# Hash-masked attention with a channel mix: the opening rearranged head by head, pair 1 turned by TensorE, and the plan of hand-overs shifted

## The chip, the cores and the metric

The kernel runs on one core of one Trainium2 chip. The time is the device time of one execution in microseconds (us). Every kernel was run several times; medians are given with the lowest and highest run. The kernel before takes 291.65 us (three runs, 291.47 to 292.93).

Each execution also has a label, fast or slow. For a kernel on one core the label only says whether that execution was more than 1.5% above the fastest one of the same kernel: no second die is there to compare with.

The engines are named PE (TensorE, the matmuls), PEld (its weight loads), DVE or VectorE, ACT or ScalarE, POOL or GpSimd, and SP, which only issues DMAs.

## The reference, cut to what matters

Four batches of eight heads; a head has 768 rows of 64. Each row of q and k gets 6 sign bits from a projection, and a query sees only the keys with the same six bits. The attention output feeds a channel mix with three weight matrices.

```python
q_bits = (np.einsum('bhsd,dk->bhsk', q, proj) > 0)          # 6 bits a row, k the same
mask = q_bucket[:, :, :, None] == k_bucket[:, :, None, :]
scores = np.where(mask, scale * q @ k.T, -1e9)
attn = softmax(scores) @ v                                   # (4, 8, 768, 64)
x = attn.transpose(0, 2, 1, 3).reshape(B, S, H * D)          # (4, 768, 512)
xk = mu_k * x + (1 - mu_k) * x_prev                          # x_prev: one row earlier
xr = mu_r * x + (1 - mu_r) * x_prev
out = sigmoid(xr @ w_r) * (np.maximum(xk @ w_k, 0) ** 2 @ w_v)
```

## The kernel before

The kernel works through 16 pairs of heads, four pairs to a batch. q and k of a pair are split into a high and a low fp16 part (`hi_part`, `lo_part`), turned so that the 64 columns lie on partitions (by PE for pair 0, by DMA after that), and the bits are computed from the turned rows with small matmuls (`bits_strip`). Each bit, times a large mark, is then written as an extra row under the 64 turned rows, by a small DMA. I call these DMAs the *row copies*. The score matmul contracts over 64+6 rows, so a matching bucket gets a large constant added, and no mask is ever built. The row copies are therefore the last thing between a pair's bits and its first score matmul.

```python
def load(n, what="qkv", engines=None):      # one DMA of 384 KB for q, k or v of a pair
    ...
def turn_by_dma(n, side):
    nc.sync.dma_start_transpose(out=st[n]["tr"][:, "qk".index(side)],
        in_=st[n]["hl" + side].rearrange("p c e -> p (c e)"))
def bits_place(n):                          # the row copies: four DMAs, one queue
    bt = st[n]["bt"]
    nc.vector.tensor_scalar(out=bt, in0=bt, scalar1=2 * MARK, scalar2=None, op0=ALU.mult)
    for g in range(4):
        nc.sync.dma_start(out=rows(n, "qk"[g // 2])[D:AUG, g % 2, :],
                          in_=bt[G * g : G * g + NB, :])
def score_unit(n, i):                       # 9 units a pair: matmuls, then one exp on ACT
    ...
        nc.tensor.matmul(sc[...], rows(n, "k")[0:AUG, j, ...], rows(n, "q")[0:AUG, j, ...])
    nc.scalar.activation(s["pt"][...], sc, AF.Exp, bias=exp_bias, scale=EXP_SCALE)
```

What happens beside the nine score units of pair n is a plan by step i:

```python
def side_work(n, i):
    prev, nxt, far = n - 1, n + 1, n + 2
    # ... prev: rest of P times v at 1, x_turn at 3, x_diff at 4
        if i in (5, 6): x_mix(prev, i - 5)              # k mix, then r mix
    # ... n: P times v of head 0 at 6, 7
        if i == 0: v_sums(nxt)
        if i in (3, 4): bits_strip(nxt, i - 3)
        if i == 4: bits_place(nxt)
        if i == 5: v_mean(nxt)
        if i == 0: hi_part, lo_part, turn_by_dma of (far, "q")
        if i == 2: hi_part, lo_part, turn_by_dma of (far, "k")
        if i in (1, 5, 7): load(n + 3, "qkv"[...])
weights = [(wk_sb, moe_w_k, 0, 2), (wk_sb, moe_w_k, 2, 2), (wr_sb, moe_w_r, 0, 4),
           (wv_sb, moe_w_v, 0, 4), (wv_sb, moe_w_v, 4, 4)]
# ... in the main loop, after step 8 of pairs 0 to 4:
            if n < len(weights) and i == 8: load_weight(*weights[n])   # GpSimd queue
```

From pair 4 on the channel mix of the finished batch is fed into the same steps (`mix_items`, from step 6 of pair 4). Each step's calls stand in the program in this order.

The softmax here doesn't subtract the row's maximum and nothing guards it: scores larger than these inputs give would overflow.

## Time and profile before

| stage (first exp to first exp) | us | PE busy, us | granted clock | what it shows |
|---|---|---|---|---|
| start, to the first exp | 23.97 | | | loads, split, turn, bits, row copies in series |
| pair 0 | 19.50 | 12.53 | see below | PE waits 5.9 for the row copies of pair 1 |
| pairs 1, 2 | 11.88, 12.41 | 9.88, 8.36 | 1.00 | waits of 1.7 and 3.6 |
| pairs 3, 4 | 14.80, 15.06 | 10.19, 15.06 | 0.85, 0.59 | a wait of 3.6, then half clock |
| pairs 5, 6 | 13.95, 14.88 | 13.90, 14.86 | 1.00 | PE is full |
| pair 7 to the end | 163.4 | | 1.00 | PE is full to 257 us, then a tail |

The exps are the best milestones. ACT runs nine a pair, each 1.11 us, and PE feeds them. The busy times by window of the kernel before, one line from first exp to first exp for pairs 0 to 6 (the header names the columns; x is the count of instructions):

```profile
core 0: us, PE busy (x) PEld busy (x) DVE busy (x) ACT busy (x) POOL busy (x), PEclk, DMA share, GB/s
23.97:43.47 19.50, 12.53 (x79) 5.52 (x78) 7.63 (x13) 9.70 (x10) 7.83 (x12) 1.00 1.04 229
43.47:55.35 11.88, 9.88 (x122) 6.36 (x121) 8.74 (x20) 9.26 (x9) 3.43 (x5) 1.00 0.51 106
55.35:67.76 12.41, 8.36 (x122) 5.12 (x121) 11.65 (x21) 9.26 (x9) 7.06 (x10) 1.00 0.95 205
67.76:82.56 14.80, 10.19 (x121) 6.47 (x120) 10.59 (x21) 9.38 (x9) 5.90 (x10) 0.85 0.87 176
82.56:97.62 15.06, 15.06 (x132) 8.81 (x131) 11.19 (x20) 10.36 (x12) 7.22 (x13) 0.59 0.86 196
97.62:111.57 13.95, 13.90 (x158) 8.72 (x156) 13.45 (x30) 13.49 (x20) 4.81 (x9) 1.00 0.96 191
111.57:126.45 14.88, 14.86 (x157) 8.84 (x158) 13.73 (x30) 12.43 (x16) 4.86 (x8) 1.00 0.65 136
```

Two regimes stand side by side. From pair 5 on PE is busy for the whole of each window. Before that it is not: pairs 1 to 3 leave it 2 to 4.6 us idle each, and pair 4 is full only because its matmuls run at a clock of 0.59. What PE waits for is in the costliest groups of instructions of the page. Behind the second bar is the idle time before the group and what ended most of it:

```profile
L287 PE MATMUL sc_0_384<-tr_215 70*128 70x256 f16 (+1 forms) x3 | 1.0, 484 | 5.9 <-DMA tr_215<-bt_278 5.9
L287 PE MATMUL sc_0_987<-tr_595 70*128 70x256 f16 (+1 forms) x3 | 1.0, 485 | 3.6 <-DMA tr_595<-bt_873 3.6
```

`tr<-bt` is a row copy: the first score matmul of a pair waits for it. The clock can also be read from a single shape. Here is the tile `tr_215`, which is pair 1: number of matmuls, shortest, median and longest in ns, start of the first and last in us.

```profile
L287 PE MATMUL sc_1_399<-tr_215 x2: 635/635/635, 43.2 to 43.6; 70*128 70x512 f16 x2
L287 PE MATMUL sc_4_482<-tr_215 x2: 380/386/391, 48.4 to 48.6; 70*128 70x512 f16 x2
```

The same 512-column matmul takes 635 ns at 43 us and 380 ns at 48 us. The column PEclk says 1.00 for pair 0, but that is not a measurement: the first clock record of this trace begins at 47.2 us, and the matmuls before it took the same 635 ns as those of pair 4 under records of 0.5 (81.4 to 95.0 us). Half rate means this here, and full rate the 380 ns under records of 1.00. For the opening of this kernel the matmul durations are to be read, not PEclk.

### The profile page before, as it was taken

Reading aid. Unit: us, or ns where it says so; the run is one execution under the profiler, and the core shown is the slowest. Engines: PE = TensorE matmul, PEld = TensorE weight load, DVE = VectorE, ACT = ScalarE, POOL = GpSimd, SP = SyncE. Lnnn points to the kernel's source line nnn. Section 1 sums busy time; section 2 is a strip of 40 time slices with the busy share of each in tenths; the row PEclk is TensorE's granted clock in tenths of the full one; section 3 lists DMA queues with packets and bytes.
Section 4 is the critical chain, followed back from the end, with each engine's and each line's share of the span. In section 5 each row is a group of like instructions: output and inputs, shape, how many; then the busy total and the mean of one; then the engine's idle time right before and its main releaser. Section 6 shows DMA issues by size and latency. Waiting matters only on the chain.

```text
span 289.9 us, 6269 instructions
## 1 busy us (share of the span) xinstructions
PE 250.1 (86%) x2489; PEld 146.0 (50%) x2489; DVE 203.5 (70%) x415; ACT 196.7 (68%) x234; POOL 83.6 (29%) x141
## 2 busy tenths in 40 slices
PE   0346919777679999999999999999999999999994
PEld 0212505545354666565657665555566656555441
DVE  0650635995878899979698999787989683666321
ACT  1015517894836999887879998777899978827420
POOL 1305240725262423332333333332414230000000
PEclk9999999997965999999999999999999999999999
DMA  6207995598968894895975646878573001111022
GB/s 235 92 3 163 208 252 132 153 211 162 217 147 203 175 180 135 144 236 116 202 185 171 146 141 139 253 112 246 132 195 68 0 31 49 38 73 38 36 92 88
DMA packets 66652, 40.58 MB, mean 140 GB/s; under 512 B 48824, under 2 KB 63040, under 8 KB 66624
## 3 DMA queue, kind: packets, MB, share of 16 engines
q1 hardware_dynamic: 64064, 37.17, 52.0%
q0 software_dynamic: 2128, 2.62, 5.9%
q8 instruction: 19, 0.31, 0.5%
q10 hardware_dynamic: 432, 0.40, 0.4%
q14 instruction: 9, 0.07, 0.1%
HBM read 24.12 MB, written 6.29 MB: 105 GB/s over the span
## 4 chain that ended last, share of the span: by engine, by line
PE 75%; DVE 8%; DMA 8%; SPq 3%; ACT 3%; issue 1%; ACTq 0%; DVEq 0%
SPq L239 3%; DMA proj_113<-in_proj_dram 2%; DMA tr_215<-bt_278 2%; DMA kn_520<-in_k_dram 1%; DMA tr_215<-khl_220 1%; ACT pt_785 L295 1%; ACT pt_383 L295 1%; PE oo_1_805 L306 1%; PE oo_1_1006 L306 1%; PE oo_1_403 L306 1%; PE oo_0_329 L306 1%; DMA tr_394<-bt_672 1%; PE vp_0_3757 L409 1%; PE vp_0_2716 L409 1%; PE vp_5_3211 L409 1%
## 5 line engine op out<-in xcount | busy, mean ns | idle before, releaser
L377 PEld LDWEIGHTS <-wk_sb 128*128 128x128 bf16 x256 | 23.5, 98 | 17.2 <-issue 2.6
L196 PE MATMUL qtp_145<-ident_h,qhl_142 128*128 128x128 f16 x12 | 1.5, 312 | 9.8 <-DVE qhl_142 L177 9.8
L217 PEld LDWEIGHTS <-phi 128*32 128x32 f16 x128 | 3.6, 95 | 12.1 <-issue 10.6
L205 ACT COPY tr_141<-ktp_162 128x1536 f16<-128x1536 f16 x1 | 1.4, 1439 | 11.5 <-PE ktp_162 L196 11.5
L287 PEld LDWEIGHTS <-tr_141 70*128 70x128 f16 x24 | 2.7, 132 | 8.4 <-DMA tr_141<-bt_184 4.4
L287 PEld LDWEIGHTS <-tr_215 70*128 70x128 f16 x24 | 2.3, 115 | 8.8 <-DMA tr_215<-bt_278 6.6
L287 PE MATMUL sc_0_384<-tr_215 70*128 70x256 f16 (+1 forms) x3 | 1.0, 484 | 5.9 <-DMA tr_215<-bt_278 5.9
L287 PEld LDWEIGHTS <-tr_595 70*128 70x128 f16 x24 | 2.6, 131 | 7.0 <-DMA tr_595<-bt_873 4.0
L196 PEld LDWEIGHTS <-qhl_142 128*128 128x128 f16 x12 | 1.2, 145 | 9.8 <-DVE qhl_142 L177 9.8
L295 ACT ACTIVATE pt_242<-sc_0_243,exp_bias 128x1024 bf16<-128x1024 f32 x1 | 1.1, 1113 | 7.3 <-PE sc_0_243 L287 7.3
L171 DVE TENSOR_SCALAR qhl_254<-qn_236 128x768 f16<-128x768 f32 x1 | 0.6, 561 | 7.3 <-DMA qn_236<-in_q_dram 7.3
L268 POOL TENSOR_TENSOR va_229<-vn_176,mean_227 128x384 bf16<-128x384 f32 x2 | 1.9, 994 | 11.8 <-DVE mu_sb L151 11.8
L306 PEld LDWEIGHTS <-pt_242 128*128 128x128 bf16 x72 | 4.5, 135 | 1.2 <-issue 1.1
L287 PEld LDWEIGHTS <-tr_394 70*128 70x128 f16 x24 | 2.1, 107 | 5.9 <-DMA tr_394<-bt_672 4.0
L295 ACT ACTIVATE pt_383<-sc_0_384,exp_bias 128x1024 bf16<-128x1024 f32 x1 | 1.1, 1113 | 5.9 <-PE sc_0_384 L287 5.9
L320 DVE TENSOR_SCALAR rc_1_440<-oo_1_403 128x6 f32<-128x6 f32 x1 | 0.2, 165 | 6.6 <-PE oo_1_403 L306 6.6
L287 PE MATMUL sc_0_243<-tr_141 70*128 70x256 f16 (+1 forms) x3 | 1.0, 484 | 4.3 <-DMA tr_141<-bt_184 4.3
L143 DVE CAST phi<-proj_113 128x32 f16<-128x32 f32 x1 | 0.2, 181 | 6.1 <-DMA proj_113<-in_proj_dram 6.1
L306 PEld LDWEIGHTS <-pt_785 128*128 128x128 bf16 x72 | 3.6, 116 | 1.7 <-issue 1.4
L268 POOL TENSOR_TENSOR va_318<-vn_182,mean_316 128x384 bf16<-128x384 f32 x2 | 1.9, 996 | 7.9 <-DVE mean_316 L261 7.9
L287 PE MATMUL sc_0_987<-tr_595 70*128 70x256 f16 (+1 forms) x3 | 1.0, 485 | 3.6 <-DMA tr_595<-bt_873 3.6
L306 PEld LDWEIGHTS <-pt_584 128*128 128x128 bf16 x72 | 3.6, 116 | 0.7 <-issue 0.3
(1736 smaller groups left out, 988.2 us busy)
## 6 DMA issues: line engine op xcount, KB each, us to landing
wk_sb<-in_moe_w_k_dram POOLq DMA_DIRECT2D x2, 512.0 KB, 7.0
wv_sb<-in_moe_w_v_dram POOLq DMA_DIRECT2D x2, 512.0 KB, 8.7
wr_sb<-in_moe_w_r_dram POOLq DMA_DIRECT2D x1, 512.0 KB, 8.2
qn_109<-in_q_dram SPq DMA_DIRECT2D x1, 384.0 KB
kn_111<-in_k_dram ACTq DMA_DIRECT2D x1, 384.0 KB
vn_176<-in_v_dram SPq DMA_DIRECT2D x1, 384.0 KB
qn_178<-in_q_dram SPq DMA_DIRECT2D x1, 384.0 KB
kn_180<-in_k_dram SPq DMA_DIRECT2D x1, 384.0 KB
```

Source lines behind the costliest of these rows:

```text
L143: nc.vector.tensor_copy(phi, proj2)
L171: nc.vector.tensor_scalar(out=hl[:, :, 0:D], in0=src, scalar1=SCALE, scalar2=None, op0=ALU.mult)
L196: nc.tensor.transpose(tp[:, c // per, (c % per) * P : (c % per + 1) * P], st[n]["hl" + side][:, c, :], ident_h,)
L205: nc.scalar.copy(dst, tp[:, :, 0:S])
L217: nc.tensor.matmul(bp[G * g : G * (g + 1), 0:STRIP], (phi, plo)[w], rows(n, "qk"[g // 2])[:, g % 2, sp * STRIP : (sp + 1) * STRIP], start= ...
L239: nc.sync.dma_start(out=rows(n, "qk"[g // 2])[D:AUG, g % 2, :], in_=bt[G * g : G * g + NB, :],)
L268: nc.gpsimd.tensor_tensor(out=va[:, j, :, 0:D], in0=loaded[n, "v"][:, j], in1=mean[:, j * D : (j + 1) * D].unsqueeze(1).to_broadcast([P, N ...
L287: nc.tensor.matmul(sc[:, at - i * UNIT : upto - i * UNIT], rows(n, "k")[0:AUG, j, jc * P : (jc + 1) * P], rows(n, "q")[0:AUG, j, q0 : q0 + ...
L295: nc.scalar.activation(s["pt"][:, i * UNIT : end], sc, AF.Exp, bias=exp_bias, scale=EXP_SCALE)
L306: nc.tensor.matmul(s["oo", j][:, ic * W : (ic + 1) * W], s["pt"][:, at : at + P], s["va"][:, j, jc, :], start=(jc == 0), stop=(jc == NSC - 1),
L377: nc.tensor.matmul(kp[:, 0:STRIP], wk_sb[:, dc, fc * P : (fc + 1) * P], mixed[b * NPB + dc, 0][:, sp * STRIP : (sp + 1) * STRIP], start=(d ...
L409: nc.tensor.matmul(vp, k2s[b, fc, sp][:, col : col + P], wv_sb[:, fc, :], start=(fc == 0), stop=(fc == NFC - 1),)
```

## The change

The intent: bring the first exp forward by working on pair 0 head by head, take the wait for the first DMA transposes out by letting PE turn pair 1, and set each hand-over between engines two steps apart, so that from pair 3 on the row copies come six steps ahead of their use and lie ahead of the loads. (Those of pair 2 stay at step 4, and those of pair 1 move back to step 6 of pair 0.) The sums of v come a block ahead. Some of VectorE's work (the r mixes of the first four pairs) moves into pair 5. Cut to its core:

```diff
-    load(0, "qk", (nc.sync, nc.scalar))
+    load_by_head(0, "qk", (nc.sync, nc.scalar))
 ...
-    def bits_place(n):
+    def bits_place(n, engines, heads=(0, 1)):
 ...                                             # k rows on a second queue
-            nc.sync.dma_start(
-                out=rows(n, "qk"[g // 2])[D:AUG, g % 2, :],
+                engines[i].dma_start(
+                    out=rows(n, side)[D:AUG, j, :], in_=bt[G * g : G * g + NB, :]
 ...                                             # squares of two k strips at a time
-        nc.vector.tensor_tensor(out=k2, in0=kr, in1=kr, op=ALU.mult)
+        if h == 1:
+            k2 = k2_pool.tile([P, 2, STRIP], BF16, ...)
+            nc.vector.tensor_tensor(out=k2, in0=kr, in1=kr, op=ALU.mult)
 ...                                             # side_work gives way to a plan
+        if n > 0:
+            i = (0, 5, 3, 2)[n] if n < 4 else 2
+            at(n - 1, i, 0.42, bits_strip, n, 0)
+            at(n - 1, i + 1, 0.42, bits_strip, n, 1)
+            at(n - 1, i + 1, 0, bits_place, n, (nc.sync, nc.gpsimd))
+            i = (0, 0, 5, 4)[n] if n < 4 else 3
+            for x, side in enumerate("qk"):
+                if n > 1:
+                    at(n - 2, i + 2 * x, 0, split if n > 2 else split_lo, n, side)
+                    at(n - 2, i + 2 * x, 0, turn_by_dma, n, side)
+        if n > 2:
+            at(n - 3, 6 if n > 3 else 7, 0, load, n, "qk")
+            at(n - 3, 8, 0, load, n, "v")
+        at(n + 1, 5, 0, x_mix, n, 0)
+        if n < NPB:
+            at(NPB + 1, 2 * n + 1, 0, x_mix, n, 1)
+        else:
+            at(n + 1, 8, 0, x_mix, n, 1)
 ...                                             # weights: step 0 instead of 8
+    at(0, 0, 0, load_weight, wk_sb, moe_w_k, 0, 2)
+    at(1, 0, 0, load_weight, wk_sb, moe_w_k, 2, 2)
+    at(2, 0, 0, load_weight, wr_sb, moe_w_r, 0, 4)
+    at(3, 0, 0, load_weight, wv_sb, moe_w_v, 0, 4)
+    at(4, 0, 0, load_weight, wv_sb, moe_w_v, 4, 4)
 ...                                             # pair 1 by PE, within pair 0
+        for j in range(2):
+            at(0, 2 * "qk".index(side) + j, 0.35, bring, 1, side, j, nc.vector.tensor_copy)
+            at(0, 2 * "qk".index(side) + j, 0, lambda k: copies[k](), (1, side, j))
```

In the opening, `split`, `bring` (turn by PE), the copy out of PSUM and the bits of pair 0 are named head by head, ACT does some of the high parts and copies, and the projection is prepared only when the first bits need it.

## The prediction

> **What bounds the kernel now.** It works through 16 pairs of heads; a pair is 9 score units, each ending in an exp of 1.11 us on ACT. The busy times by window show two regimes.
>
> From the first exp of pair 5 (97.6 us) to 257 us PE is busy 100%, a pair takes 14 to 15 us, and the chain of waits is almost pure PE; in the tail (to 289.9 us) PE is busy 28.8 of 32.9 us.
>
> Before that PE waits. First exps of pairs 0 to 5, by the timeline: 23.97, 43.47, 55.35, 67.76, 82.56, 97.62 us. Exps spaced 1.0 us need about 9.5 us a pair, so pairs 0 to 4 (73.7 us) lose some 25 us:
>
> - Start: proj lands at 7.0 us and holds VectorE; then q split, turn, copy, k split, turn, copy (1.44 us on ACT), bits, row copies on one queue (0.67 us each), in series. First score 22.89 us.
> - Row copies end PE's idle time before pairs 1 to 4: 5.9, 1.7, 3.6, 3.6 us (groups of waits).
> - Clock: up to 46 us a 512-column score matmul takes 635 ns, later 380, and 635 again after the 3.6 us gaps; the granted clock is 0.5 from 82 to 94 us. [...]
>
> **The change.** Start: loads by head, half-size splits and copies, ACT doing q copies and the hi parts of pairs 1 and 2, the table load hidden, proj off the front of VectorE's order, row copies on two queues. I estimate the first exp at 16 us (8 earlier); pair 2's loads now precede the row copies, so not earlier. Pair 1 by PE: +24 transposes (about 0.107 us each at half rate, 2.6 us) and four VectorE copies of about 0.5 us, against two DMA transposes (22.5 to 28.3 us). Row copies from pair 3 on come six steps ahead instead of four, before their block's loads. Four r mixes (0.41 + 0.56 us or more each) move from pairs 1 to 4 into pair 5.
>
> **Sum (estimates).** Pair 0: 12.5 us, partly at half rate (was 19.5). Pairs 1 to 3: 11 us each (were 11.9, 12.4, 14.8); not 9.5, because the DMA share there was already 0.51, 0.95, 0.87 and must rise[...]. Pair 4 at full clock: 11 (was 15.1). First exp of pair 5: 72.5 instead of 97.6, 25 us gained. Pair 5 gives back about 2: VectorE was busy 13.45 of its 13.95 us and gets 3.9 us of mixes, less what pairing k2 saves (single squares 0.35 us). From pair 6 on nothing: PE bound, same work, same tail. So 291.65 - 23.5 = 268 us. Range 259 to 279. Faster by over 2%: 0.95, within 2%: 0.04, slower: 0.01.
>
> **What would show it.** First exp near 16 us; 380 ns score matmuls within pair 0; no PE idle above 1.5 us for row copies before pairs 2 to 4; granted clock near 1.0 from 60 us on; pair 5 at 16 us with VectorE over 95% busy; pairs 6 to 15 and the tail unchanged.
>
> **What would make it wrong.** DMA saturating pairs 1 to 4 (share over 1.0, splits waiting for loads), so that gaps and half clock return: 278. ACT's order at the start (hi parts of pair 2 wait for loads) delaying the first exp to 19 us. Or better: pairs 1 to 4 at exp pace and a warm pair 0, 259. Deferred mixes could stall PE on PSUM banks in pair 5 by more than 2 us.

Two passages are cut out of it, each marked: the sentence that followed the measured clocks, and the reason given for the rise of the DMA share. No term of the sum is cut: 291.65 - 23.5 comes to 268 us, and that the share must rise stands as the author's estimate. Two figures in it can be found in the trace of the kernel before: its transposes by PE start 0.107 us apart, and the table load is the 1.28 us of ACT at 2.47 us.

## The result, and the profile after

The changed kernel takes 277.64 us (three runs, 276.03 to 281.25) against 291.65. Its ratio to the kernel before is 0.948, 95% interval 0.939 to 0.957. Here and below a ratio is the mean time of one kernel's fast runs over that of the other's of the same rounds, so it is not quite the ratio of the medians I quote. The result is correct. Unchanged copies of the kernel were run again as controls and were slower: 282.17 (276.50 to 283.86) and 282.05 (279.29 to 283.60), ratios 0.957 and 0.960. So the change is worth some 9 to 14 us, and the kernel it gives varies by several us from run to run, more than the kernel before did.

The busy times by window of the kernel after, pairs 0 to 6. The profiled execution took 281.25 us, the longest of the three; the two controls' profiles took 282.30 and 283.30. No execution near 276 us of this kernel was profiled, so the stages below add up to a smaller gain (10.4 us) than the medians do (14).

```profile
16.35:31.71 15.36, 14.84 (x106) 8.65 (x107) 7.97 (x17) 9.92 (x10) 4.40 (x6) 1.00 0.22 41
31.71:45.47 13.76, 13.14 (x120) 7.77 (x119) 8.24 (x18) 9.60 (x10) 5.67 (x12) 1.00 0.82 186
45.47:58.63 13.16, 9.12 (x121) 5.49 (x121) 8.25 (x18) 9.48 (x11) 8.07 (x14) 0.95 1.11 204
58.63:72.81 14.18, 13.22 (x120) 7.73 (x119) 8.42 (x18) 9.70 (x9) 4.37 (x10) 0.56 0.84 172
72.81:85.24 12.43, 10.23 (x131) 6.19 (x131) 8.82 (x19) 10.50 (x12) 6.14 (x12) 1.00 1.07 207
85.24:99.34 14.10, 14.10 (x161) 9.04 (x160) 11.89 (x24) 13.46 (x20) 5.27 (x10) 1.00 0.55 140
99.34:116.62 17.28, 14.76 (x156) 8.64 (x157) 16.69 (x33) 12.47 (x16) 7.64 (x12) 1.00 0.59 141
```

Put beside the prediction's sum, stage by stage:

| stage | before | predicted | after |
|---|---|---|---|
| start | 23.97 | 16 | 16.35 |
| pair 0 | 19.50 | 12.5 | 15.36 |
| pairs 1 to 3 together | 39.09 | 33 | 41.10 |
| pair 4 | 15.06 | 11 | 12.43 |
| pairs 5 and 6 together | 28.83 | 31 | 31.38 |
| pair 7 to the end of the span | 163.4 | the same | 162.8 |

The start came as predicted, and the rest of the program did not change. The whole shortfall lies in pairs 0 to 4. They were to give 17 us (73.7 to 56.5) and gave 4.8 (73.65 to 68.89) in this execution, 5.9 and 5.7 in the controls. Pairs 1 to 3 even became 2 us longer here (and 1.9 shorter in both controls), in spite of all the rearranging of their hand-overs.

Three things stand in the windows. PE was busy 14.84 of 15.36 us in pair 0 and yet slow. Pair 3 has a clock of 0.56. And in pair 6 VectorE is busy 16.69 of 17.28 us, while PE is not full. The tiles of pairs 1 and 2 after the change tell when the clock rose:

```profile
L309 PE MATMUL sc_7_585<-tr_191 x2: 618/626/634, 42.0 to 42.4; 70*128 70x512 f16 x2
L309 PE MATMUL sc_8_621<-tr_191 x3: 269/270/377, 43.8 to 44.0; 70*128 70x256 f16 x2, 70*128 70x512 f16 x1
```

In this execution all of pair 0 and nearly all of pair 1 ran at half rate, until 43.7 us, where the first clock record begins. The next records say half rate from 57.3 to 71.0 us, then full to the end. The timeline of the kernel after shows what came before that fall (start, length in us, then in brackets the idle time before it and what ended it):

```profile
49.36 0.81 POOL L172 DMA_DIRECT2D wr_sb<-in_moe_w_r_dram  x1
...
51.06 1.49 SPq L262 DMA_DIRECT2D tr_540<-bt_690  x2
...
51.63 1.00 POOL L262 DMA_DIRECT2D tr_540<-bt_690  x2 [1.12 <-ACT pt_628 L317]
...
57.49 1.03 PE L309 MATMUL sc_0_827<-tr_540 70*128 70x512 f16 x3 [3.15 <-DMA tr_540<-bt_690]
```

The row copies of pair 3 were issued early, at 51.06 and 51.63 us, when PE still had about three us of work: it fell idle at 54.34. They landed at 57.45. The weight `wr` had been issued on the same GpSimd queue at 49.36. (A weight is 1 MB of float32 in DRAM and 512 KB of bf16 where it lands.) The page's DMA issues (KB each, then the median time from issue to landing) let the pairs be compared; `tr_213` is pair 2, `tr_1128` pair 6:

```profile
wr_sb<-in_moe_w_r_dram POOLq DMA_DIRECT2D x1, 512.0 KB, 7.9
...
tr_213<-bt_508 POOLq DMA_DIRECT2D x2, 9.0 KB, 2.3
tr_540<-bt_690 POOLq DMA_DIRECT2D x2, 9.0 KB, 5.8
tr_732<-bt_888 POOLq DMA_DIRECT2D x2, 9.0 KB, 2.7
tr_930<-bt_1086 POOLq DMA_DIRECT2D x2, 9.0 KB, 5.1
tr_1128<-bt_1316 POOLq DMA_DIRECT2D x2, 9.0 KB, 1.7
```

The same 9 KB took 1.7 to 2.7 us, or 5.1 and 5.8 (medians of two; the later copy of pair 4 took 3.66 with no weight under way). The two slow ones were issued 2.3 and 2.8 us after a 512-KB weight on that queue; those of pairs 2 and 4 were issued 6.0 and 6.5 us after one, when it was nearly in. 49.36 plus 7.9 is 57.3, which is just where the rows of pair 3 came out. Both flights are in the chain that ended last, although PE stood idle for only 0.26 us before the first scores of pair 5:

```profile
51.63 5.82 DMA tr_540<-bt_690
...
79.21 5.20 DMA tr_930<-bt_1086
```

In pair 6 the timeline shows two of VectorE's squares of a pair of strips at 1.35 us each, and behind them a wait of PE for a normalised output (`ob`), which VectorE had to produce:

```profile
103.09 1.35 DVE L413 TENSOR_TENSOR k_0_3_1_1522<-kr_2_1_1514 128x768 bf16<-128x768 bf16 x1
...
106.65 0.51 PE L357 MATMUL ot_1623<-ident_b,ob_1482 128*128 128x128 bf16 x6 [2.41 <-DVE ob_1482 L346]
```

Most such squares take 0.55 us (the timeline has one at 99.00 us, for instance). The two slow ones overlap with work of GpSimd on SBUF: the subtraction of v's mean from 101.65 to 104.03 us and the sums of v, whose first part ran from 103.98 to 105.29. Each ended 0.41 us after the GpSimd work that it overlapped. That the overlap slowed them is the author's reading of these times; no run here took the one from the other. Two single squares had mostly taken 0.35 us each before, so where the pairing was to save VectorE time, it cost some here. But the two slow squares alone did not make PE wait: in experiment 4 they took 1.35 us again, and PE was full.

### The profile page after: what moved, and what is told of

Read it like the earlier page. It is cut to its first block, busy times and chain, and to the rows that moved or that the text cites. A ratio compares the mean times of both kernels' runs of the same rounds, so it can differ in the third digit from the quotient of the medians.

```text
span 279.4 us, 6281 instructions
## 1 busy us (share of the span) xinstructions
PE 254.2 (91%) x2496; PEld 149.5 (53%) x2513; DVE 196.8 (70%) x391; ACT 201.8 (72%) x240; POOL 97.9 (35%) x171
## 4 chain that ended last, share of the span: by engine, by line
PE 76%; DVE 11%; DMA 9%; issue 2%; SPq 0%; ACT 0%; POOLq 0%; DVEq 0%
DMA tr_540<-bt_690 2%; DMA tr_930<-bt_1086 2%; DMA tr_930<-khl_949 2%; DMA kn_583<-in_k_dram 2%; DMA qn_109<-in_q_dram 1%; PE oo_1_842 L328 1%; PE oo_1_446 L328 1%; PE vp_4_4323 L436 1%; PE oo_0_958 L328 1%; PE vp_5_4342 L436 1%; PE vp_1_3827 L436 1%; PE vp_1_2814 L436 1%; PE vp_0_3732 L436 1%; PE vp_5_3204 L436 1%; PE vp_5_2170 L436 1%
## 5 line engine op out<-in xcount | busy, mean ns | idle before, releaser
L309 PEld LDWEIGHTS <-tr_540 70*128 70x128 f16 x24 | 2.6, 129 | 7.3 <-DMA tr_540<-bt_690 3.5
L218 PE MATMUL tpq_0_161<-ident_h,qhl_158 128*128 128x128 f16 x6 | 0.8, 307 | 4.8 <-DVE qhl_158 L201 4.8
L328 PEld LDWEIGHTS <-pt_245 128*128 128x128 bf16 x72 | 4.5, 135 | 1.2 <-issue 1.1
L290 POOL TENSOR_TENSOR va_305<-vn_145,mean_303 128x384 bf16<-128x384 f32 x2 | 1.9, 989 | 8.3 <-DVE mean_303 L283 8.3
L290 POOL TENSOR_TENSOR va_1495<-vn_1022,mean_1493 128x384 bf16<-128x384 f32 x2 | 2.4, 1205 | 7.0 <-DVE mean_1493 L283 7.0
L309 PEld LDWEIGHTS <-tr_157 70*128 70x128 f16 x24 | 2.8, 137 | 3.4 <-issue 3.3
L236 PEld LDWEIGHTS <-plo 128*32 128x32 f16 x128 | 3.9, 100 | 1.0 <-issue 0.8
L309 PEld LDWEIGHTS <-tr_191 70*128 70x128 f16 x24 | 2.6, 130 | 3.4 <-issue 2.6
L290 POOL TENSOR_TENSOR va_2261<-vn_1771,mean_2259 128x384 bf16<-128x384 f32 x2 | 2.5, 1262 | 4.7 <-DVE mean_2259 L283 4.7
L290 POOL TENSOR_TENSOR va_3295<-vn_2812,mean_3293 128x384 bf16<-128x384 f32 x2 | 2.5, 1260 | 4.7 <-DVE mean_3293 L283 4.7
L290 POOL TENSOR_TENSOR va_2009<-vn_1507,mean_2007 128x384 bf16<-128x384 f32 x2 | 2.4, 1208 | 5.0 <-DVE mean_2007 L283 5.0
L290 POOL TENSOR_TENSOR va_3043<-vn_2548,mean_3041 128x384 bf16<-128x384 f32 x2 | 2.4, 1206 | 4.9 <-DVE mean_3041 L283 4.9
L328 PEld LDWEIGHTS <-pt_430 128*128 128x128 bf16 x72 | 3.6, 116 | 0.9 <-issue 0.6
L290 POOL TENSOR_TENSOR va_1759<-vn_1235,mean_1757 128x384 bf16<-128x384 f32 x2 | 2.4, 1204 | 4.8 <-DVE mean_1757 L283 4.8
L328 PEld LDWEIGHTS <-pt_826 128*128 128x128 bf16 x72 | 3.6, 115 | 0.9 <-issue 0.6
L290 POOL TENSOR_TENSOR va_3566<-vn_3055,mean_3564 128x384 bf16<-128x384 f32 x2 | 2.4, 1206 | 4.7 <-DVE mean_3564 L283 4.7
L328 PEld LDWEIGHTS <-pt_628 128*128 128x128 bf16 x72 | 3.6, 116 | 0.8 <-issue 0.6
L290 POOL TENSOR_TENSOR va_2536<-vn_2021,mean_2534 128x384 bf16<-128x384 f32 x2 | 2.4, 1206 | 4.7 <-DVE mean_2534 L283 4.7
L290 POOL TENSOR_TENSOR va_2793<-vn_2281,mean_2791 128x384 bf16<-128x384 f32 x2 | 2.4, 1208 | 4.5 <-DVE mean_2791 L283 4.5
```

What stands on the lines that cost most here:

```text
L218: nc.tensor.transpose(tp[:, c], st[n]["hl" + side][:, j * NSC + c, :], ident_h)
L236: nc.tensor.matmul(bp[G * g : G * (g + 1), 0:STRIP], (phi, plo)[w], rows(n, side)[:, j, sp * STRIP : (sp + 1) * STRIP], start=(w == 0), st ...
L290: nc.gpsimd.tensor_tensor(out=va[:, j, :, 0:D], in0=loaded[n, "v"][:, j], in1=mean[:, j * D : (j + 1) * D].unsqueeze(1).to_broadcast([P, N ...
L309: nc.tensor.matmul(sc[:, at - i * UNIT : upto - i * UNIT], rows(n, "k")[0:AUG, j, jc * P : (jc + 1) * P], rows(n, "q")[0:AUG, j, q0 : q0 + ...
L328: nc.tensor.matmul(s["oo", j][:, ic * W : (ic + 1) * W], s["pt"][:, at : at + P], s["va"][:, j, jc, :], start=(jc == 0), stop=(jc == NSC - 1),
```

## The experiments

All are edits of the kernel after. Medians are of all runs of the kernel. The calls ran on three chips (experiments 1 to 4, then control 1 and 5 to 7, then control 2 and 8 to 10), where the kernel before took 291.61, 290.80 and 292.31 us. Most times that were expected were missed: experiments 1, 2, 5, 6, 7 and 8 came out 4 to 18 us slower than the theory that each one tested had it.

| kernel | median (lowest to highest), us | ratio to before |
|---|---|---|
| weights four steps later | 287.35 (286.05 to 292.48) | 0.982 |
| all row copies on SP's queue | 279.27 (278.35 to 281.92) | 0.957 |
| 17 filler matmuls at the start | 276.99 (272.22 to 280.07) | too few fast runs |
| r mixes back in their pairs | 275.40 (273.10 to 279.84) | 0.940 |
| control 1, unchanged | 282.17 (276.50 to 283.86) | 0.957 |
| no weights in pairs 1 to 4 | 276.24 (275.46 to 277.69) | 0.949 |
| that, and r mixes back | 275.01 (271.06 to 276.69, and one of 615.17) | 0.938 |
| both, and 31 filler matmuls | 271.31 (270.79 to 272.38) | 0.933 |
| control 2, unchanged | 282.05 (279.29 to 283.60) | 0.960 |
| all of that, rows of pair 1 earlier | 283.42 (278.26 to 289.37) | 0.956 |
| the same without filler | 283.70 (278.08 to 287.47) | 0.954 |
| pair 1 turned by DMA | 277.34 (274.03 to 282.05) | 0.945 |

The length of the pairs in the profiled executions, in us. From pair 7 on these kernels agree within 0.2 us a pair, so everything is decided before. Where a control differs from the first profile of the same kernel, that is the variation of the kernel itself. Each line is one execution.

| kernel | first exp | 0 | 1 | 2 | 3 | 4 | 5 | 6 |
|---|---|---|---|---|---|---|---|---|
| after | 16.4 | 15.4 | 13.8 | 13.2 | 14.2 | 12.4 | 14.1 | 17.3 |
| control 1 | 15.7 | 14.8 | 13.9 | 12.8 | 10.5 | 15.7 | 13.9 | 20.3 |
| control 2 | 16.3 | 15.2 | 13.9 | 12.7 | 10.6 | 15.6 | 13.9 | 20.4 |
| weights four steps later | 16.3 | 15.8 | 10.3 | 17.5 | 15.1 | 14.0 | 16.1 | 16.2 |
| row copies on SP | 15.3 | 15.8 | 13.9 | 11.6 | 11.0 | 14.1 | 13.9 | 19.1 |
| 17 fillers | 15.1 | 13.9 | 14.2 | 11.1 | 14.4 | 12.5 | 13.9 | 20.3 |
| r mixes back | 16.2 | 14.9 | 12.7 | 14.2 | 13.0 | 15.6 | 13.9 | 14.7 |
| no weights in 1 to 4 | 16.1 | 15.7 | 10.3 | 11.9 | 10.8 | 13.2 | 13.9 | 19.6 |
| both and 31 fillers | 14.5 | 15.3 | 10.3 | 11.5 | 11.1 | 13.2 | 13.9 | 16.3 |
| rows of pair 1 earlier | 15.0 | 9.7 | 27.7 | 9.7 | 11.1 | 13.3 | 14.4 | 17.8 |
| the same without filler | 15.7 | 11.2 | 26.4 | 11.6 | 10.9 | 13.2 | 15.2 | 16.2 |
| pair 1 by DMA | 16.0 | 14.2 | 11.6 | 14.3 | 11.3 | 13.9 | 13.9 | 19.1 |

### 1. Are the weights in the way of the row copies? Issue them four steps later

The first theory was that a weight issued at step 0 delays the row copies issued at step 3, and that moving it behind them cures it. The rival was that the DMA engines lack the time in pairs 1 to 4 whatever the order.

```diff
-    at(0, 0, 0, load_weight, wk_sb, moe_w_k, 0, 2)      # and four more like it
+    at(0, 4, 0, load_weight, wk_sb, moe_w_k, 0, 2)
```

> The weight loads move from step 0 of pairs 0 to 4 to step 4, behind the row copies of their block. Theory A (the k row copies sit in GpSimd's DMA queue behind a weight load of 1 MB issued 2.3 to 2.7 us earlier): the k row copies for pairs 3 and 5 land in 1.7 to 2.7 us instead of 5.8 and 5.1, PE's 3.15 us wait before pair 3 goes, the granted clock stays near 1.0 from 56 to 70 us, and the time falls by 4 to 7 us, to about 271. Rival B (all 16 DMA engines are full with loads and transposes, whatever queue): landing still 5 us, time within 1.5 us of 277.

It became slower: 287.35 us, about 10 more than the kernel after. Against the later controls it is 5 us, and its shortest run (286.05) is longer than their longest (283.86). The row copies were now in time. But the transposes of the next pair came after the weight and were late, and PE waited for them in their turn. In the timeline, within pair 2:

```profile
47.49 0.34 PE L236 MATMUL bp<-tr,phi 128*32 128x384 f16 x1 [2.77 <-DMA tr<-qhl]
```

The clock was at half rate from 48.1 to 58.4 and from 65.2 to 78.9 us. So this order is not the cure: the weight only changed who waits for it.

### 2. Is it the second queue? All row copies on SP's queue

Half of the row copies share GpSimd's queue with the weights. If that queue is the trouble, SP's queue is the cure.

```diff
-            at(n - 1, i + 1, 0, bits_place, n, (nc.sync, nc.gpsimd))
+            at(n - 1, i + 1, 0, bits_place, n, (nc.sync, nc.sync))
```

> All row copies from pair 1 on go through SyncE's queue, as in the kernel before; the weights stay at step 0 on GpSimd's queue. Theory A: the row copies no longer stand behind the weights, but behind the block's loads (1.15 MB issued some 5 us earlier) and need 4 issues of 0.7 us; they land about 3.5 to 4.5 us after the first issue, the wait before pair 3 shrinks to under 1 us, time 271 to 275. Rival B: still 5 to 6 us, time 277 or a little more.

The wait before pair 3 shrank to 1.04 us, from 3.15 (3.05 and 3.07 in the controls), with `wr` still under way until 55.85 us:

```profile
55.90 1.04 PE L309 MATMUL sc<-tr 70*128 70x512 f16 x5 [1.04 <-DMA tr<-bt]
```

The clock stayed up from 43.4 to 104.8 us, and pairs 2 and 3 took 11.6 and 11.0 us (12.8 and 10.5, 12.7 and 10.6 in the controls). But the time is not shown to be better: 279.27, and 0.957 is also the ratio of control 1. So the queue matters to how long these copies wait behind a weight, and is not all of it: in the kernel before, whose row copies are on SP's queue too, the wait of 5.9 us before pair 1 ended at 42.39 us, just as a weight issued among them at 36.21 landed (42.34).

### 3. Is the half clock at the start the loss? Keep PE busy with filler

```diff
+    heat = wv_sb[:, 0, :]
+    nc.vector.memset(heat, 0.0)
+    def keep_busy(k):                    # 512-column matmuls whose result nobody reads
+        hp = bank(f"hp{k}")
+        for _ in range(k):
+            nc.tensor.matmul(hp, heat[:, 0:P], heat, start=True, stop=True)
+    keep_busy(8)                         # ahead of the first turn
     ...
+    keep_busy(9)                         # while head 1 of pair 0 is prepared
```

> 17 matmuls of 512 columns without use fill the waits of PE in the start (1.4 to 4.8 us and 8.8 to 11.6 us). Theory C (pairs 0 and 1 take 15.4 and 13.8 us because PE is at half rate until 43.7 us): the score matmuls show 380 ns in pair 0, pair 0 takes 11 to 12 us and pair 1 10 to 11, the first exp stays at 16.4 us, and the time falls by 4 to 7 us. Rival D (the pace of pairs 0 and 1 is set by the hand-overs between DVE, PE and ACT): warm matmuls, but pairs 0 and 1 stay above 13 us each and the time within 1.5 us of 277. If the clock does not warm, the run decides nothing on this.

The clock rose at 6.2 us, but it fell back at 16.4, and pair 0 took 13.9 us. Four runs spread from 272.22 to 280.07 us and only one counts as fast, so there is no ratio. That is inconclusive. It shows that 17 of these matmuls did not hold the clock. They may have brought it up early (6.2 us), but without filler it also came up for a while, at 8.6 us, in control 1.

### 4. What do the delayed r mixes cost? Put them back

```diff
-        if n < NPB:
-            at(NPB + 1, 2 * n + 1, 0, x_mix, n, 1)
-        else:
-            at(n + 1, 8, 0, x_mix, n, 1)
+        at(n + 1, 8, 0, x_mix, n, 1)
```

> The r mixes of pairs 0 to 3 go back to their own blocks (step 8 of the next pair) instead of pair 5. Theory E (the four deferred mixes overload VectorE in pair 5; its backlog holds PE 2.4 us at the turn in pair 6): pair 6 takes 14.6 to 14.9 us instead of 17.3, pairs 1 to 4 grow by under 0.5 us each as VectorE is busy only 8 of 13 us there, time falls by about 2 us to 275. Rival F (pair 6 is long for another reason, a DMA or the pairing of k2): pair 6 stays at 17 us.

Pair 6, in the busy times by window:

```profile
100.55:115.24 14.69, 14.69 (x158) 8.71 (x157) 13.95 (x25) 12.47 (x16) 7.07 (x12) 1.00 0.59 144
```

PE is full again and VectorE has 13.95 us of work instead of 16.69. Pair 6 went from 17.28 us (20.3 in the controls) to 14.69. That the mixes were put where VectorE had no room, and cost 2.6 us or more there, is shown by this pair. The time went to 275.40, ratio 0.940 against 0.948, with intervals that overlap (0.934 to 0.946, and 0.939 to 0.957). That the mixes are nearly free in the earlier pairs, where VectorE is busy 8 to 9 of 13 to 14 us, is argued and not shown: pairs 1 to 4 took 55.5 us together in this profile, 53.5 in the kernel after, and 52.9 and 52.8 in the controls, but at half clock for 27.3, 25.6 and 22.5 us of that, so the two causes are not told apart.

### 5. Control, and no weights at all in pairs 1 to 4

Experiment 1 had left one theory standing: whatever stands in line with a weight in pairs 1 to 4 comes late. A weight alone is about a quarter of the DMA time of such a pair: I add up its packets to about 3.4 us of all 16 engines. And the windows of the kernel after have a DMA share of 0.82, 1.11, 0.84, 1.07 there. The cure would then be to take the weights out. They are not needed before the channel mix, which begins in pair 4 with `wk` alone.

```diff
-    at(1, 0, 0, load_weight, wk_sb, moe_w_k, 2, 2)
-    at(2, 0, 0, load_weight, wr_sb, moe_w_r, 0, 4)
-    at(3, 0, 0, load_weight, wv_sb, moe_w_v, 0, 4)
-    at(4, 0, 0, load_weight, wv_sb, moe_w_v, 4, 4)
+    at(0, 3, 0, load_weight, wk_sb, moe_w_k, 2, 2)
+    at(5, 0, 0, load_weight, wr_sb, moe_w_r, 0, 4)
+    at(5, 4, 0, load_weight, wv_sb, moe_w_v, 0, 4)
+    at(5, 7, 0, load_weight, wv_sb, moe_w_v, 4, 4)
```

The control is the kernel after without an edit.

> The changed kernel itself, unchanged, as a control on the same chip as the next three. Both theories: median 276 to 279, and single runs that spread over some 5 us (276.0, 277.6, 281.3 so far) because the half-rate periods of PE in pairs 0 to 4 fall differently; the pairs from 7 on as before (14.6, 14.2, 14.0, 14.0).

> Both loads of wk go into pair 0 (steps 0 and 3, where the DMA share is 0.22), wr and both loads of wv into pair 5 (share 0.55): pairs 1 to 4 have no weight load. Theory B (in pairs 1 to 4 the DMA engines are full, so a weight of about 3.5 us of all 16 engines delays whatever is behind it: row copies, or the transposes when it was moved to step 4): no wait of PE above 1.5 us for row copies or turned rows in pairs 1 to 4, pairs 2 to 4 take 10 to 11.5 us each, row copies on GpSimd's queue land in under 3 us, time 268 to 272. Rival G (it is the loads and transposes of the pairs themselves, not the weights): gaps of 2 to 4 us before pairs 3 and 5 stay, time 276 to 278.

The control took 282.17 us, this one 276.24. All six runs of it lie within 2.2 us, where the control's spread over 7.4, and five of the control's six are longer than all of them. By the fast runs alone (two of the control's six) the intervals overlap: 0.945 to 0.954, and 0.948 to 0.965. Pair 1 of the control in the busy times by window, and then pairs 1 to 4 of this kernel:

```profile
30.48:44.37 13.89, 13.28 (x120) 7.94 (x119) 8.23 (x18) 9.59 (x9) 4.95 (x11) 0.56 0.79 184
```

```profile
31.84:42.17 10.33, 9.57 (x120) 6.17 (x119) 6.75 (x14) 9.23 (x9) 4.54 (x10) 0.83 0.65 172
42.17:54.04 11.87, 8.68 (x121) 5.31 (x121) 8.89 (x22) 9.51 (x10) 5.33 (x10) 1.00 0.80 190
54.04:64.84 10.80, 8.43 (x120) 5.19 (x119) 7.98 (x17) 9.29 (x10) 5.32 (x10) 1.00 0.72 182
64.84:78.07 13.23, 10.38 (x132) 6.37 (x132) 9.79 (x23) 10.53 (x12) 5.60 (x11) 1.00 0.72 173
```

The DMA share is 0.65 to 0.80, no gap of PE in them is longer than 1.52 us, and the clock stays up from 35.8 to 100.7 us. The row copies of pairs 2 to 5 on GpSimd's queue land in 1.67 to 3.44 us (under 3 was expected). Pairs 1 to 3 take 33.0 us together, which is what I had predicted for the change itself, and 37.2 in the control. So the weights were the cause of the late row copies: moved within the pairs they held up other transfers (experiment 1), and without them no transfer held PE up for more than 1.52 us. Not all of the 4.2 us is theirs, though: 3.6 lie in pair 1, where the waits before it were alike (1.48 us here, 1.65 in the control) and the clock was back after 3.4 us here and after 13.65 in the control. Why it came back sooner is not shown. A gap that the weights made was also followed by a slow clock (3.15 us, and then 13.65 us at half rate, in the first profile; 3.4 us in the controls), so it may have cost twice; that the gap is what lowered the clock is the author's reading and was not shown. The time missed the 268 to 272 us that were expected; the mixes still lay in pair 5, and pair 6 took 19.6 us, nearly as in the control (20.3). That the spells of slow clock also make the kernel's time wander fits the narrow spread here, but was not tested by itself.

### 6. Both cures together

```diff
     # the weights as in experiment 5, and the r mixes as in experiment 4
```

> As e5_weights_pair5, and the r mixes back in their own blocks as in e4_mix_back. Theories B and E together: pair 6 at 14.7 us, pairs 2 to 4 at 10 to 11.5; time 2 to 3 us under e5_weights_pair5, about 267. If the DMA engines are the limit of pairs 1 to 4 rather than VectorE, the added 1 us of VectorE work in each costs nothing; if VectorE is the limit once the weights are gone, the gain of e4_mix_back (2.6 us in pair 6) is given back in pairs 1 to 4.

The median was 275.01 us, the fast runs' mean 272.9, ratio 0.938. Its interval, 0.931 to 0.944, just does not touch that of experiment 5 (0.945 to 0.954), but only three of its six runs count as fast. One of the six executions took 615.17 us, and it was the profiled one. There the 512-column matmuls of the channel mix took 823 ns on average, PE was busy 98% of the span and no clock record exists. The group in its page:

```profile
L436 PE MATMUL vp<-wv_sb,k 128*128 128x512 bf16 x192 | 123.7, 823 | 0.0
```

That is neither of the two rates (380 and 635 ns). Its five other executions took 271.06 to 276.69 us with the same code, so this says nothing of the edit, and I leave it out. For this kernel there is thus no usable profile.

### 7. Both cures, and filler long enough to hold the clock

```diff
     # the weights as in experiment 5, the r mixes as in experiment 4
+    keep_busy(9)                                          # ahead of the first turn
     ...
+    keep_busy(13)                                         # while head 1 is prepared
     ...
+    keep_busy(5)                                          # before pair 0
+    plan[0].insert(0, (0, lambda: keep_busy(4)))
```

> As e6_weights_mix, with useless 512-column matmuls in PE's waits of the start (9, 13, 5 and 4 of them). Theory C: the clock is full from about 6 us through pair 0 and 1; pairs 0 and 1 take 11 to 12 and 10 to 11 us; the time falls another 4 to 6 us to about 262, and single runs spread less. Rival D: pairs 0 and 1 stay over 13 us with warm matmuls. If the clock falls back to half rate within pair 0, as in e3_keep_busy at 16.4 us, the gain is 1 to 2 us.

This is the best version: 271.31 us (270.79 to 272.38), ratio 0.933, interval 0.929 to 0.937. Against the kernel after as it was first measured that is 6 us, against the control 11. It beats both kernels. The clock rose at 4.9 us and held to 25.3. The fast means of this and the kernel without filler, 271.5 and 272.9, have intervals that overlap, so what the filler is worth is not separated.

And pair 0 still took 15.3 us, although its score matmuls ran at full rate. The timeline shows why:

```profile
20.01 0.76 POOL L172 DMA_DIRECT2D wk_sb<-in_moe_w_k_dram  x1
...
23.38 1.05 POOL L262 DMA_DIRECT2D tr<-bt  x2 [2.62 <-PE sc L309]
24.15 1.49 SPq L262 DMA_DIRECT2D tr<-bt  x2
...
28.73 1.87 PE L309 MATMUL sc<-tr 70*128 70x512 f16 x5 [5.29 <-DMA tr<-bt]
```

PE finished the scores of pair 0 at 23.4 us and then waited 5.29 us for the row copies of pair 1. In the kernel after this wait had been hidden under the slow clock: there PE was at work, slowly, until it began on pair 1 at 30.6 us. So pair 0 had two limits, half clock and hand-over, and taking one away showed the other. Part of this second limit was made by the experiment: `wk`, which it had moved into pair 0 (20.01 us), landed at 25.63, and the row copies on its queue took 4.4 and 4.5 us; in the kernel after, with no weight near, they took 1.7 and 1.9.

The weights were not free in pair 5 either. Pair 6 took 16.3 us here and 14.7 in experiment 4, with the same mixes. The DMA share of pairs 5 and 6 was 0.95 and 0.96 instead of 0.53 and 0.59, and PE waited for a transpose:

```profile
94.67 0.34 PE L236 MATMUL bp<-tr,phi 128*32 128x384 f16 x3 [1.26 <-DMA tr<-khl]
```

### 8. Control, and the rows of pair 1 earlier

```diff
     # experiment 7, and:
-            i = (0, 5, 3, 2)[n] if n < 4 else 2           # step of the bits
+            i = (0, 4, 3, 2)[n] if n < 4 else 2
-            i = (0, 0, 5, 4)[n] if n < 4 else 3           # step of the transposes
+            i = (0, 0, 6, 4)[n] if n < 4 else 3
-    at(0, 3, 0, load_weight, wk_sb, moe_w_k, 2, 2)
+    at(0, 7, 0, load_weight, wk_sb, moe_w_k, 2, 2)
-    at(5, 4, 0, load_weight, wv_sb, moe_w_v, 0, 4)
-    at(5, 7, 0, load_weight, wv_sb, moe_w_v, 4, 4)
+    at(5, 2, 0, load_weight, wv_sb, moe_w_v, 0, 4)
+    at(5, 4, 0, load_weight, wv_sb, moe_w_v, 4, 4)
```

> The changed kernel unchanged, again as a control on the same chip as the next three: 276 to 284, spread as before.

> e7_all_busy with the bits and row copies of pair 1 one step earlier (steps 4 and 5 of pair 0), ahead of the first DMA transpose of pair 2 and of the second load of wk, and wv 2 and 3 steps earlier in pair 5. In e7_all_busy PE ran warm through pair 0, finished its scores at 23.4 us, and then waited 5.29 us for the row copies of pair 1. Theory H (that wait is the queue: row copies issued 24.15 us behind a transpose and a weight): the wait falls under 1.5 us, pair 0 takes 10 to 11 us, the clock stays full to the end, pair 6 falls from 16.3 to about 15, time 265 to 267. Rival J (the row copies of pair 1 are late because VectorE gets to the bits late): the wait only moves, time 270 to 271.

Pair 0 did what the theory of two limits asks for. In the busy times by window:

```profile
15.01:24.74 9.73, 9.00 (x109) 5.54 (x108) 7.76 (x16) 9.26 (x9) 3.83 (x6) 1.00 0.32 60
```

9.73 us, the pace of the exps, with a wait of 0.64 us for the rows of pair 1. But the time was 283.42 us, no better than the control (282.05). Pair 1 lost it all: 27.7 us. Here is its timeline:

```profile
26.46 4.00 SPq L210 DMA_TRANSPOSE tr<-khl  x1
26.64 0.77 POOL L172 DMA_DIRECT2D wk_sb<-in_moe_w_k_dram  x1
...
43.50 0.51 PE L236 MATMUL bp<-tr,phi 128*32 128x384 f16 x3 [15.35 <-DMA tr<-khl]
```

The transpose of k of pair 2 had slipped behind the loads of q and k of pair 3 and met the weight `wk`. From its issue at 26.46 to its landing at 43.45 us it took 17 us, and PE stood still for 15.35. In the packet records of the trace, the small packets (below 300 bytes), most of them the transposes', took 69 ns on average in that stretch, at most 2533, against 22 ns later in the same run. The expectation had not foreseen this. The edit moved the bits, the transposes and the weight at once, so which of these moves made the stall is not separated.

### 9. The same without filler

```diff
     # experiment 8 without the keep_busy calls
```

> e8_rows1_early without the useless matmuls. Theory C (the clock of pairs 0 and 1): pair 0 takes 14 to 16 us at half rate, time 4 to 6 us over e8_rows1_early, and single runs spread more. Rival: with the DMA waits gone PE warms by itself, time within 1.5 us of e8_rows1_early.

283.70 us, the same as with filler within the spread. Pair 0 took 11.2 us instead of 9.7, its clock rose by itself at 19.7 us, and pair 1 took 26.4 us with a gap of 13.76 us: the late transpose again. So with early rows, and the clock as it came, pair 0 took 11.2 us instead of 15.2 in control 2. Not all of that need be the rows: the clock came up at 26.7 us in control 2, and the weights and mixes were moved as well. The filler gave some 1.5 us there and 0.7 in the start, in one execution each. The stall of pair 1 does not come from the filler.

### 10. The rival for pair 1: turn it by DMA after all

The change turned pair 1 by PE at 24 transposes. The rival says that this was no gain.

```diff
         split_lo(1, side)
-        for j in range(2):
-            at(0, 2 * "qk".index(side) + j, 0.35, bring, 1, side, j, nc.vector.tensor_copy)
-            at(0, 2 * "qk".index(side) + j, 0, lambda k: copies[k](), (1, side, j))
+        turn_by_dma(1, side)
```

> The changed kernel with pair 1 turned by DMA again (the rest of the change as it is). Theory K (turning pair 1 by PE is needed: the DMA transposes of pair 1 would land after step 5 of pair 0): PE waits 2 us or more for them in pair 0, time up by 2 to 5 us. Rival L (with PE at half rate in pair 0, its 24 transposes, 2.6 us by estimate, and four VectorE copies cost as much as they save): pair 0 falls from 15 to about 13 us and the time is the same within 2 us or lower.

277.34 us against 282.05 of control 2. The fast runs' means are 276.3 and 281.3 with ratios whose intervals do not touch (0.939 to 0.951, and 0.954 to 0.966). So the rival is right in this: turning pair 1 by PE was not a gain in the kernel after. (Against the first measurement of the kernel after, 0.939 to 0.957, the intervals overlap.) Pairs 0 and 1 in the busy times by window, first control 2 and then this kernel:

```profile
16.32:31.53 15.21, 13.32 (x106) 8.01 (x107) 7.97 (x17) 9.89 (x9) 4.74 (x7) 0.95 0.30 57
31.53:45.43 13.90, 13.29 (x120) 7.95 (x119) 8.24 (x18) 9.59 (x9) 4.95 (x11) 0.56 0.82 184
```

```profile
16.02:30.23 14.21, 11.02 (x81) 5.20 (x80) 5.74 (x13) 9.68 (x10) 4.68 (x7) 0.62 0.66 121
30.23:41.86 11.63, 9.48 (x122) 5.97 (x121) 7.97 (x18) 9.36 (x9) 4.95 (x10) 0.89 0.99 219
```

PE has 2.3 us less work in pair 0 (11.02 us instead of 13.32), mostly at half rate, and VectorE 2.2 us less, and pair 0 is 1 us shorter. Pair 1 is 2.3 us shorter, with a clock of 0.89 instead of 0.56. (The 0.95 of control 2 in pair 0 is not a measurement: its first clock record begins at 26.7 us.) How much of the 5 us is the work and how much the luck of the clock these runs do not settle.

## Why the prediction was right or wrong

The time was predicted at 268 us in 259 to 279 and measured at 277.64, near the upper end: faster, as said, with a gain of 14 us where 23.5 were predicted. That it lies within the range is partly luck: two later controls of the same kernel, at 282, lie above it. Point by point:

- **"I estimate the first exp at 16 us (8 earlier)": right.** 16.35 us, 7.6 earlier; 15.7 and 16.3 in the controls.
- **"Pair 0: 12.5 us, partly at half rate": too short.** 15.36, and all of it at half rate. The expected mark, "380 ns score matmuls within pair 0", did not come: 606 to 634 ns until 42 us in the tiles. Experiments 7, 8 and 9 showed that the clock was one of two limits: with a full clock until its scores were done, pair 0 still took 15.3 us because of the row copies of pair 1 (delayed there by a weight of the experiment's own), and only with earlier rows and that weight out of the way 9.7.
- **"Pairs 1 to 3: 11 us each" and "Pair 4 at full clock: 11": this is the step that failed.** They took 41.10 and 12.43 us instead of 33 and 11 (37.2 and 15.7 in the controls). The prediction looked at the DMA share (0.51, 0.95, 0.87), said that it "must rise", and still assumed hand-overs in time. It rose to 0.82, 1.11, 0.84, 1.07 and the row copies of pair 3 came 3.15 us late. Half clock followed for 13.65 us. Experiment 5 shows the cause of the late copies: without the weights in these pairs the wait was gone, and pairs 1 to 3 took 33.0 us together, of which some is the clock of pair 1. Pair 4 takes 13.2 there, so 11 was too short for it in any case: the channel mix begins within it.
- **The sum for pairs 0 to 4, a gain of 17 us, was mis-sized**: 4.8 us in the first profile. With the start right at 8, that is the whole miss of the profiled execution. "No PE idle above 1.5 us for row copies before pairs 2 to 4" and "granted clock near 1.0 from 60 us on" were the marks for it, and both failed (3.15 us; 0.56 in pair 3). The case was named under "what would make it wrong" with 278 us; it should have been the main case, since the shares were on the table.
- **"Pair 5 gives back about 2 ... VectorE over 95% busy": right in size and mechanism, wrong in place.** Pair 5 took 14.10 us with VectorE busy 11.89. The cost came in pair 6, at 17.28 us with VectorE busy 16.69 (97%). The squares taken in pairs, which were to save time there, took 1.35 us twice in that window instead of 0.55. Experiment 4 confirms that the delayed mixes were the cause: without them pair 6 took 14.69 us, with the same two slow squares. In the controls the cost was higher, 20.3 us, with the clock at half rate for 6.8 us after a wait of 2.57 us.
- **"From pair 6 on nothing: PE bound, same work, same tail": right from pair 7 on**, 163.4 us before and 162.8 after.

What stays open: what makes PE's clock rise and fall (the last section has what the traces show of this); what made pair 1 of experiment 8 stall; why turning pair 1 by DMA was 5 us better and how much of it is clock; what makes pair 4 take 15.6 us in the controls beyond their half rate from 74.5 to 81.4 us (control 2). A version not run would be experiment 8 with both `wk` loads at the start of pair 0 and the k transpose of pair 2 ahead of the loads. If pair 1 then keeps its 10.3 us, I would expect 5 us less than experiment 7; that is an estimate from pair 0's 15.3 and 9.7 us and nothing that was shown.

## What to carry to other kernels

In stages with a DMA share near 1 (0.82 to 1.11 here), moving a weight within the stage only changed who waited (experiment 1, 287.35 us): look for bytes that are not needed there at all, here 512-KB weights that could wait for a stage bound by PE, and check each hand-over again after the move. The new place has a price too: pair 6 grew from 14.7 to 16.3 us when the weights came into pair 5. Short waits of PE were followed here by a slow clock (3.15 us by 13.65 us at half rate in the kernel after, 2.57 us by 6.8 in control 2), so a kernel whose time wanders by several us from run to run is worth reading for such gaps; that the wait is the cause was not shown. When a stage stays the same length after its apparent limit is gone, look for a second limit of the same length, as the row copies under the slow clock of pair 0.

## What the traces show of the clock and of transfers side by side

- **A busy PE and the rise of the clock.** In the kernel after PE was busy 14.84 of 15.36 us in pair 0 and 13.14 of 13.76 in pair 1 by the profile, and its 512-column matmuls stayed at 606 to 634 ns until 43.7 us. In the controls, with the same code, the clock came up at 8.6 and 26.7 us. So a busy share near 1 in the profile was not enough here, and what is enough these runs do not show.
- **Waits of PE and the fall of the clock.** In the kernel before, two waits of 3.6 us were followed by 3.41 and 13.65 us at half rate. In the kernel after 3.15 us was followed by half rate and 2.41 us was not; but 2.57 us was followed by half rate in both controls, and with pair 1 turned by DMA the clock fell from 43.0 to 60.1 us with no single gap above 1.72 us in the 25 us ahead of it. So the length of the longest gap did not decide it here.
- **The clock records.** Before the first clock record the profile reads as full rate while matmuls take 635 ns. One execution here, of 615.17 us with 823-ns matmuls, has no clock record at all and reads as full rate throughout.
- **A transpose beside ordinary DMAs.** All results were correct. In experiment 8 one transpose beside two loads and a weight took 17 us from issue to landing, with small packets of 69 ns on average instead of 22, and PE stood for 15.35 us.
- **A small transfer behind a large one.** The 9-KB row copies took 1.7 to 2.7 us (medians by pair in the kernel after), and 5.1 to 5.8 us when issued 2.3 to 2.8 us after a 512-KB weight on their queue.
